# Score columns of a head group dealt to other rounds, and one corner sum read straight from PSUM

## The chip, the cores and the metric

The kernel runs on one core of a Trainium2 chip. The metric is the device time of one execution in microseconds. The profile is one execution taken by the hardware profiler. Its engines are TensorE (PE, with its weight loads as PEld), VectorE (DVE), ScalarE (ACT), GpSimd (POOL) and SyncE (SP).

## The reference

For 8 batches of 8 heads with 576 tokens and head dimension 64, a causal attention with a forget gate is computed, and its output (4608 tokens by 512) goes through a two-layer network with a gelu between.

```python
scores = scale * np.matmul(q, k.transpose(0, 1, 3, 2))
cum = np.cumsum(np.log(np.clip(f, 0.0001, 1.0)), axis=-1)
scores = np.where(causal, -1e9, scores + cum[:, :, :, None] - cum[:, :, None, :])
attn = softmax(scores)
x = np.matmul(attn, v).transpose(0, 2, 1, 3).reshape(B * S, H * D)
h = x @ w_in                       # 512 -> 2048
out = gelu_tanh(h) @ w_out         # 2048 -> 512
```

## The kernel before

**Order of the work.** All work is written out by hand as words in tables (FRONT, SECOND, STEADY, FLUSH, LAST, from L75); each engine gets its instructions in that order. S is a score round, M a mask on POOL, m the same mask on DVE, D the softmax denominators, V the value product, VW and vw the weighting of the values on POOL and DVE, CL a small copy on DVE, LQ and LK loads, TQ and TK transposes on DVE. I, i, Q, E and e are parts of the first layer, F and f steps of the second layer, T and UW sums for both. The tables put F and f steps between the attention's words, so that PE has work while ACT, DVE and POOL finish what the attention needs next.

**Attention.** Four heads of a batch form a head group, `i` from 0 to 15. Keys lie on the partitions, queries on the columns. A score tile for head group i >= 2 has 1536 columns per head, dealt in three rounds of 512 (`rounds`, L50). The list `pieces` (L51) says which columns belong to which key tile: (key tile, first column, first query, number of queries). There are 5 key tiles of 128 keys; the last one is half full. Its 64 keys ("high") share columns 0 to 63 with the 64-column piece "low", which holds the first 64 keys for the first 64 queries in the other half of the partitions. Before the change key tile 0 stands at columns 64 to 575, so that it has 448 columns in round 0 and 64 in round 1.

A round (`scores`, L259) multiplies, for each half `c` of the head dimension and each piece, the four heads one after another, each in its own 32 rows of PE (L277), and ends with two exponentials on ACT into `pt`, 128x1024 each (L285). `mask` (L287) then zeroes the columns above the diagonal with POOL instructions (L291); `mask_by_product` (L311) does it with DVE products by a triangle (L321). `product` (L325) multiplies `pt` by the weights (`denominators`) or by the values (`attn_out`), in the order of key tile 0, low, 1, 2, 3, high (L347). `pt` has two buffers. Head groups 0 and 1 use other tables (`split_pieces`).

**Second layer.** Tokens go in 9 chunks of 512. Chunk 0 is a plain product (`mlp_out`). Chunks 1 to 8 take seven products of blocks instead of eight (`seven_products`, L586). Two PSUM banks, pa and pb, take them in turn; some products add onto what a bank holds. A product that is needed twice is kept in SBUF by a copy on DVE (`keep`, L615, in a pool of three buffers, copy at L617). `result` (L619) sums two parts into an output tile (L624, three buffers) and sends it out on SP's queue. The corner for output block (1,1) stands behind the fifth product:

```python
def corner():
    keep("v4", pa)
    result(1, 1, kept["p7"], kept["v4"])
```

After it come a product into pb and then the last product, which adds onto pa in chunks 1 to 7. In the last chunk (8, `last`) the final product goes to new banks and `piece` adds `kept["v4"]` to it.

Of the kernel before, what the change touches and what calls it, by code (L numbers as in the profile page):

```python
# [16 lines left out]
def kernel(  # L17
# [10 lines left out]
    nc = tc.nc  # L28
# [21 lines left out]
    rounds = [(0, 512), (512, 512), (1024, 512)]  # L50
    pieces = [  # L51
        ("low", 0, 0, 64),
        (0, 64, 64, 512),
        (1, 576, 128, 448),
        (2, 1024, 256, 320),
        (3, 1344, 384, 192),
        ("high", 0, 512, 64),
    ]
# [62 lines left out]
    def many(n, shape, dtype, name):  # L121
        return [singles.tile(shape, dtype, name=f"{name}{i}") for i in range(n)]
# [31 lines left out]
    causal = many(2, [128, 128], BF16, "causal")  # L154
# [8 lines left out]
    for u in range(4):  # L163
        if u not in wsum:
            n = 3 * len([x for x in wsum if x not in UNIT_LIST])
            wsum[u] = [last_w[:, 512 * (n + k):512 * (n + k + 1)].rearrange("p (d n) -> p d n", n=HC) for k in range(3)]

    def gelus(c, ft=0, n=HF):

        half = last_g[ft // HF] if c == NCH - 1 else gT[:, HF * (ft // HF):HF * (ft // HF) + HF]  # L170
        return half[:, ft % HF:ft % HF + n]

    def sums_of(c):
        return (last_s[0], last_s[1], g4) if c == NCH - 1 else (g1, g2, g4)
# [112 lines left out]
    def mask(i, r, keys=None):  # L287
        p = pt[i % 2]

        def keep(x, pattern):  # L290
            nc.gpsimd.affine_select(  # L291
                out=x, in_=x, compare_op=ALU.is_ge,
                fill=0.0, base=0, pattern=pattern, channel_multiplier=-1)

        if i < 2:
            for (key, col, n) in diagonals(r, keys):
                keep(p[:, :, col:col + n], [[0, 4], [1, n]])
            return
        if r == 0:
            keep(p[0:64, :, 0:64], [[0, 4], [1, 64]])  # L300
            keep(p[64:128, :, 0:128].rearrange("p h (b x) -> p h b x", x=64), [[0, 4], [0, 2], [1, 64]])
        for (key, col, q0, nq) in pieces:
            if key in (keys or (1, 2, 3)) and rounds[r][0] <= col < rounds[r][0] + 512:
                keep(p[:, :, col:col + 128], [[0, 4], [1, 128]])

    def diagonals(r, keys):

        return [(4 if key == "high" else key, col, min(nq, 128)) for (key, col, q0, nq) in split_pieces[r]
                if q0 == (512 if key == "high" else 128 * key) and (not keys or (4 if key == "high" else key) in keys)]

    def mask_by_product(i, r, keys=None):  # L311
        p = pt[i % 2]
        if i < 2:
            todo = [(0, col, n) for (key, col, n) in diagonals(r, keys)]
        else:
            todo = [(1 if key == "low" else 0, col, 128) for (key, col, q0, nq) in pieces
                    if (not keys or key in keys) and q0 == 128 * (0 if key == "low" else 9 if key == "high" else key)
                    and rounds[r][0] <= col < rounds[r][0] + 512 and key != 0]
        did = None
        for (m, col, n) in todo:  # L320
            did = nc.vector.tensor_mul(p[:, :, col:col + n], p[:, :, col:col + n],  # L321
                                 causal[m][:, 0:n].unsqueeze(1).to_broadcast([128, 4, n]))
        return did

    def product(i, groups, spare, part=None):  # L325
# [243 lines left out]
    def gelu_sums(half, which=(1, 3, 2, 4), c=0):  # L569

        n = HF // 2
        f0 = slice(n * half, n * half + n)
        g1, g2, g4 = sums_of(c)
        top, low = gelus(c, n * half, n), gelus(c, HF + n * half, n)
        a11, a12, a21, a22 = top[:, :, 0:HC], low[:, :, 0:HC], top[:, :, HC:CH], low[:, :, HC:CH]
        for k in which:
            if k == 1:
                nc.vector.tensor_add(g1[:, f0], a21, a22)
            if k == 2:
                nc.vector.tensor_sub(g2[:, f0], g1[:, f0], a11)  # L580
            if k == 3:
                nc.vector.tensor_sub(a21, a11, a21)
            if k == 4:
                nc.vector.tensor_sub(g4[:, f0], a12, g2[:, f0])

    def seven_products(c):  # L586

        r0, last = CH * c, c == NCH - 1
        g1, g2, g4 = sums_of(c)
        top, low = gelus(c), gelus(c, HF)  # L590
        a11, a12, d1, a22 = top[:, :, 0:HC], low[:, :, 0:HC], top[:, :, HC:], low[:, :, HC:]
        w11, w3 = w_out_sb[:, 0:HF, 0:HD], w_out_sb[:, 0:HF, HD:]
        w21, w22 = w_out_sb[:, HF:, 0:HD], w_out_sb[:, HF:, HD:]

        def multiply(ps, x, w, first, then, ns=range(2), cols=(0, HD)):
            for n in ns:
                for j in range(HF):
                    width = 32 if by_columns else 128
                    for c0 in range(0, 128, width):
                        nc.tensor.matmul(ps[c0:c0 + width, n, cols[0]:cols[1]],  # L600
                                         x[:, j, 128 * n + c0:128 * n + c0 + width],
                                         w[:, j, cols[0]:cols[1]],
                                         start=(first and n == ns[0] and j == 0), stop=(j == HF - 1),
                                         skip_group_check=True)
                    if n == ns[-1] and j == HF - 1:
                        then()
                    yield

        def bank():
            return psM.tile([128, 2, HD], FP32, name="ps_w", tag="m")  # L610

        kept = {}
        copy = nc.scalar.copy if c in ON_ACT else nc.vector.tensor_copy

        def keep(name, ps):  # L615
            kept[name] = snap_pool.tile([128, 2, HD], FP32, name="snap", tag="snap")
            copy(kept[name], ps)  # L617

        def result(i, j, x, y=None):  # L619
            st = ostage_pool.tile([128, 2, HD], FP32, name="o_st", tag="o")  # L620
            if y is None:
                copy(st, x)
            else:
                nc.vector.tensor_add(st, x, y)  # L624
            nc.sync.dma_start(
                out=out[r0 + HC * i:r0 + HC * (i + 1), HD * j:HD * (j + 1)].rearrange("(n p) d -> p n d", p=128),
                in_=st)

        def first_corner():
            result(0, 0, pb, kept["p1"])  # L630
            gelu_sums(1, (3, 4), c)

        def corner():
            keep("v4", pa)
            result(1, 1, kept["p7"], kept["v4"])

        def piece(ps, n, cols):
            st = v_nat[0][:, 0, 4 * n:4 * n + 4, :].rearrange("p h d -> p (h d)")
            s = slice(*cols)
            nc.vector.tensor_add(st[:, s], ps[:, n, s], kept["v4"][:, n, s])  # L640
            eng = nc.scalar if cols[0] else nc.sync
            eng.dma_start(out=out[r0 + 128 * n:r0 + 128 * n + 128, HD + cols[0]:HD + cols[1]], in_=st[:, s])

        pa, pb = bank(), bank()
        yield from multiply(pa, a11, w11, True, lambda: keep("p1", pa))
        yield from multiply(pb, a12, w21, True, first_corner)
        yield from multiply(pa, g2, u2, False, lambda: keep("v2", pa))
        yield from multiply(pb, d1, w3, True, lambda: keep("p7", pb))
        yield from multiply(pa, g1, u1, False, corner)
        yield from multiply(pb, a22, u4, False, lambda: result(1, 0, pb, kept["v2"]))  # L650
        if not last:
            yield from multiply(pa, g4, w22, False, lambda: result(0, 1, pa))
            return
        for n, cols in ((0, (0, HD)), (1, (0, HD // 2)), (1, (HD // 2, HD))):
            ps = bank()
            yield from multiply(ps, g4, w22, True, lambda: piece(ps, n, cols), (n,), cols)
# [94 lines left out]
    def load_values(b, half):  # L751
# [9 lines left out]
        "S": lambda i, r: scores(i, r),  # L761
        "H": lambda i, r, g: scores(i, r, ((2 * g, 2 * g + 1),)),
        "M": lambda i, r, *keys: mask(i, r, keys),
        "m": lambda i, r, *keys: mask_by_product(i, r, keys),
        "D": denominators,
        "V": lambda i, x, *part: attn_out(i, x, False, *part),
# [92 lines left out]
```

## Time and profile before

| | |
|---|---|
| runs | 323.99, 325.89, 326.36 us (median 325.89) |
| span of the profiled execution | 324.3 us; no other time of it is given |
| PE busy | 310.0 us (96%), 5337 matmuls |
| DVE busy | 241.7 us (75%), 374 instructions |
| ACT busy | 212.6 us (66%) |
| POOL busy | 107.0 us (33%) |
| TensorE clock granted | 1.000 of full speed |

The span runs from the first to the last instruction. A busy time is the time in which the engine has at least one instruction under way. Matmuls overlap on PE, so the mean of one matmul is longer than the distance between two starts. Lines like L277 are lines of the kernel before.

### The profile page before, as it was taken

Reading aid. Unit: us, or ns where it says so; the run is one execution under the profiler, and the core shown is the slowest. Engines: PE = TensorE matmul, PEld = TensorE weight load, DVE = VectorE, ACT = ScalarE, POOL = GpSimd, SP = SyncE. Lnnn points to the kernel's source line nnn. Section 1 sums busy time; section 2 is a strip of 40 time slices with the busy share of each in tenths; the row PEclk is TensorE's granted clock in tenths of the full one; section 3 lists DMA queues with packets and bytes.
Section 4 is the critical chain, followed back from the end, with each engine's and each line's share of the span. In section 5 each row is a group of like instructions: output and inputs, shape, how many; then the busy total and the mean of one; then the engine's idle time right before and its main releaser. Section 6 shows DMA issues by size and latency. Waiting matters only on the chain.

```text
span 324.3 us, 11816 instructions
## 1 busy us (share of the span) xinstructions
PE 310.0 (96%) x5337; PEld 221.2 (68%) x5337; DVE 241.7 (75%) x374; ACT 212.6 (66%) x242; POOL 107.0 (33%) x145
## 2 busy tenths in 40 slices
PE   0799989999999999999999999999999999999996
PEld 0557844454677667776788877767776786788785
DVE  3664307998989978779876998599885866597574
ACT  4495667686766786678667876877587743846610
POOL 8868507253111405510752056305610150000000
PEclk9999999999999999999999999999999999999999
DMA  6999999577034951395119610981001011010202
GB/s 117 232 155 165 196 250 217 139 160 143 8 67 88 227 116 36 76 213 107 36 40 211 143 40 6 206 183 35 7 32 67 17 35 53 16 50 2 99 33 98
DMA packets 47490, 33.41 MB, mean 103 GB/s; under 512 B 29776, under 2 KB 42192, under 8 KB 47440
## 3 DMA queue, kind: packets, MB, share of 16 engines
q0 software_dynamic: 9632, 15.99, 28.4%
q1 hardware_dynamic: 37664, 16.60, 18.9%
q8 instruction: 41, 0.67, 0.8%
q14 instruction: 9, 0.07, 0.1%
q10 hardware_dynamic: 144, 0.07, 0.1%
HBM read 36.85 MB, written 9.44 MB: 143 GB/s over the span
## 4 chain that ended last, share of the span: by engine, by line
PE 82%; DMA 6%; POOL 4%; ACT 4%; DVE 2%; issue 1%; POOLq 0%; DVEq 0%
PE ps_w L600 30%; PE ps_h L395 19%; PE po L347 9%; PE ps_q L520 8%; PE ps_s L277 8%; DMA w_out_sb<-in_moe_w_out_dram 4%; PE ps_u L468 4%; PE pso L667 4%; DMA q_c<-in_q_dram 2%; ACT pt L285 2%; POOL pt L291 1%; POOL w_out_sb L201 1%; POOL v_nat L185 1%; POOL w_in_sb L197 1%; PE cum_ps L721 1%
## 5 line engine op out<-in xcount | busy, mean ns | idle before, releaser
L285 ACT ACTIVATE pt<-ps_s 128x1024 bf16<-128x1024 f32 (+2 forms) x100 | 93.9, 990 | 41.3 <-PE ps_s L277 37.1
L291 POOL TENSOR_SCALAR_AFFINE_SELECT pt<-pt 128x512 bf16<-128x512 bf16 (+3 forms) x65 | 40.8, 639 | 98.0 <-ACT pt L285 75.2
L395 PE MATMUL ps_h<-xT,w_in_sb 128*128 128x512 bf16 (+1 forms) x320 | 66.8, 358 | 0.3 <-ACT gT L403 0.2
L395 PEld LDWEIGHTS <-w_in_sb 128*128 128x128 bf16 x320 | 31.2, 98 | 26.7 <-issue 0.6
L600 PEld LDWEIGHTS <-gT 128*32 128x32 bf16 (+1 forms) x1216 | 44.2, 97 | 5.5 <-issue 2.2
L403 ACT ACTIVATE gT<-ps_h 128x1024 bf16<-128x1024 f32 x34 | 34.6, 1017 | 18.7 <-PE ps_h L395 18.4
L600 PE MATMUL ps_w<-w_out_sb,gT 128*32 128x256 bf16 (+1 forms) x1008 | 42.6, 273 | 0.0
L277 PE MATMUL ps_s<-qT,kT 32*128 32x64 bf16 (+5 forms) x896 | 36.3, 263 | 4.6 <-DVE qT L214 4.3
L600 PEld LDWEIGHTS <-gsum 128*32 128x32 bf16 (+1 forms) x948 | 35.5, 97 | 3.6 <-issue 1.3
L231 POOL TENSOR_TENSOR vw<-v_nat,wT 128x1280 bf16<-128x1280 f32 (+1 forms) x13 | 29.6, 2278 | 11.8 <-DMA v_nat<-in_v_dram 11.5
L536 DVE TENSOR_TENSOR usnap<-ps_q,usnap 128x1024 f32<-128x1024 f32 x15 | 17.9, 1222 | 18.6 <-PE ps_q L520 13.2
L277 PEld LDWEIGHTS <-kT 32*128 32x128 bf16 x896 | 16.5, 93 | 20.9 <-issue 11.5
L600 PE MATMUL ps_w<-usum,gsum 128*32 128x256 bf16 (+1 forms) x791 | 29.9, 273 | 0.0
L617 DVE COPY snap<-ps_w 128x512 f32<-128x512 f32 x32 | 21.8, 681 | 6.1 <-PE ps_w L600 6.0
L531 ACT ACTIVATE gT<-usnap 128x1024 bf16<-128x1024 f32 x15 | 15.8, 1054 | 12.1 <-DVE usnap L536 11.8
L379 DVE TENSOR_TENSOR xT<-po,rb 128x576 bf16<-128x576 f32 x26 | 19.5, 752 | 5.6 <-PE po L347 5.3
L347 PE MATMUL po<-pt,vw 128*32 128x64 bf16 (+4 forms) x624 | 22.4, 278 | 0.0
L214 DVE STREAM_TRANSPOSE qT<-q_c 128x576 f32<-128x576 f32 x16 | 19.8, 1247 | 2.7 <-DMA q_c<-in_q_dram 2.5
L214 DVE STREAM_TRANSPOSE kT<-k_c 128x576 f32<-128x576 f32 x16 | 19.5, 1248 | 3.1 <-DMA k_c<-in_k_dram 3.1
L347 PEld LDWEIGHTS <-vw 128*32 128x32 bf16 x672 | 14.8, 97 | 9.3 <-issue 2.8
L208 POOL DMA_DIRECT2D k_c<-in_k_dram x16 | 9.1, 569 | 33.7 <-DVE kT L214 17.4
L520 PEld LDWEIGHTS <-w_in_sb 128*128 128x128 bf16 x160 | 15.6, 98 | 2.5 <-issue 0.4
(134 smaller groups left out, 478.4 us busy)
## 6 DMA issues: line engine op xcount, KB each, us to landing
out_dram<-o_st SPq DMA_DIRECT2D x35, 256.0 KB, 2.3
k_c<-in_k_dram POOLq DMA_DIRECT2D x16, 288.0 KB, 5.2
q_c<-in_q_dram POOLq DMA_DIRECT2D x16, 288.0 KB, 6.2
v_nat<-in_v_dram SPq DMA_DIRECT2D x16, 256.0 KB, 5.3
v_nat<-in_v_dram SPq DMA_DIRECT2D x20, 128.0 KB, 4.9
v_nat<-in_v_dram POOLq DMA_DIRECT2D x8, 256.0 KB, 8.2
w_in_sb<-in_moe_w_in_dram POOLq DMA_DIRECT2D x8, 256.0 KB, 7.6
w_out_sb<-in_moe_w_out_dram POOLq DMA_DIRECT2D x4, 512.0 KB, 11.1
```

Source lines behind the costliest of these rows:

```text
L214: return nc.vector.transpose(out=dst.rearrange("p s c -> p (s c)").bitcast(FP32) .rearrange("p (t a) -> p a t", a=S // 32), in_=src.rearra ...
L231: return eng.tensor_mul(vw[i % 2][:, t0:t1], vb[:, t0:t1, h0:h0 + 4, :], wT[:, i, t0:t1, :].unsqueeze(3).to_broadcast([128, t1 - t0, 4, D]))
L277: nc.tensor.matmul(tiles[h // 2][:, h % 2, c0:c0 + nq], key_columns(i, key, h, c), qq[32 * h:32 * h + 32, q0:q0 + nq, c], start=(c == 0 an ...
L285: nc.scalar.activation(p[:, 2 * g:2 * g + 2, off:off + n], t[:, :, 0:n], AF.Exp, scale=scale)
L291: nc.gpsimd.affine_select(out=x, in_=x, compare_op=ALU.is_ge, fill=0.0, base=0, pattern=pattern, channel_multiplier=-1)
L347: nc.tensor.matmul(po[r0:r0 + w.shape[-1], 448 + q0:448 + q0 + nq], w, p[:, h, col:col + nq], start=(key in (0, "low")), stop=(key in ("lo ...
L379: nc.vector.tensor_mul(xT[:, 2 * u + x, r0 + s0:r0 + s1], po, rbs[i, part])
L395: nc.tensor.matmul(ph[:, j, n * cols:(n + 1) * cols], w_in_sb[:, dt, 128 * ft:128 * ft + 128], xT[:, dt, h0:h0 + cols], start=(dt == 0 and ...
L403: nc.scalar.activation(gelus(c, 2 * pr, 2), ph, AF.Gelu_apprx_tanh)
L520: nc.tensor.matmul(ps[:, k, HC * n:HC * n + HC], w[:, d, 128 * n:128 * n + 128], x[:, d, :], start=(first and n == 0 and d == 0), stop=(d ...
L600: nc.tensor.matmul(ps[c0:c0 + width, n, cols[0]:cols[1]], x[:, j, 128 * n + c0:128 * n + c0 + width], w[:, j, cols[0]:cols[1]], start=(fir ...
L617: copy(kept[name], ps)
```

## The change

Key tile 1 takes columns 64 to 511 and key tile 0 columns 512 to 1023, so that round 1 is key tile 0 and nothing else. Key tile 0's diagonal has a part in the low keys' half of the partitions that needs a mask: its 64 columns by 64 keys stood beside "low" in round 0 and were masked together with it; now they stand in round 1 and get a mask of 64 partitions there. Key tile 1's diagonal mask moves from round 1 to round 0. On POOL, round 0 has three masks instead of two and round 1 one smaller mask; on DVE, round 0 has two products instead of one and round 1 one smaller one. In the second layer the (1,1) corner is summed from PSUM and p7; the copy to v4 stays in the last chunk alone.

```diff
     pieces = [
         ("low", 0, 0, 64),
-        (0, 64, 64, 512),
-        (1, 576, 128, 448),
+        (1, 64, 128, 448),
+        (0, 512, 64, 512),
         (2, 1024, 256, 320),
         (3, 1344, 384, 192),
         ("high", 0, 512, 64),
...
         if r == 0:
-            keep(p[0:64, :, 0:64], [[0, 4], [1, 64]])
-            keep(p[64:128, :, 0:128].rearrange("p h (b x) -> p h b x", x=64), [[0, 4], [0, 2], [1, 64]])
+            for x in (0, 64):
+                keep(p[x:x + 64, :, 0:64], [[0, 4], [1, 64]])
+        if r == 1:
+            keep(p[64:128, :, 512:576], [[0, 4], [1, 64]])
...
-            todo = [(1 if key == "low" else 0, col, 128) for (key, col, q0, nq) in pieces
-                    if (not keys or key in keys) and q0 == 128 * (0 if key == "low" else 9 if key == "high" else key)
-                    and rounds[r][0] <= col < rounds[r][0] + 512 and key != 0]
+            todo = [(1 if key == "low" else 0, col, 64 if key in ("low", 0) else 128) for (key, col, q0, nq) in pieces
+                    if (not keys or key in keys) and key != "high"
+                    and rounds[r][0] <= col < rounds[r][0] + 512]
         did = None
         for (m, col, n) in todo:
-            did = nc.vector.tensor_mul(p[:, :, col:col + n], p[:, :, col:col + n],
-                                 causal[m][:, 0:n].unsqueeze(1).to_broadcast([128, 4, n]))
+            p0 = 64 if (i >= 2 and r == 1) else 0
+            m = 1 if p0 else m
+            did = nc.vector.tensor_mul(p[p0:, :, col:col + n], p[p0:, :, col:col + n],
+                                 causal[m][p0:, 0:n].unsqueeze(1).to_broadcast([128 - p0, 4, n]))
...
         def corner():
-            keep("v4", pa)
-            result(1, 1, kept["p7"], kept["v4"])
+            if last:
+                keep("v4", pa)
+            result(1, 1, pa, kept["p7"])
```

## The prediction

> **What bounds the kernel now.** I read the page's first part, then its chain of work, then the list of what TensorE (PE) waited for.
>
> ```profile
> PE 310.0 (96%) x5337; PEld 221.2 (68%) x5337; DVE 241.7 (75%) x374; ACT 212.6 (66%) x242; POOL 107.0 (33%) x145
> ...
> PE 82%; DMA 6%; POOL 4%; ACT 4%; DVE 2%; issue 1%; POOLq 0%; DVEq 0%
> ```
>
> PE is busy for 310.0 of 324.3 us and carries 82% of the chain that ended last. DVE, which the second half of the change relieves, has 2% of that chain.
>
> ```profile
> PE ps_lt L700 <- POOL utri_f masks.py:66: 4.7, 1, 4.7
> PE ps_s L277 <- DVE qT L214: 4.3, 1, 4.3
> PE pso L667 <- DMA w_out_sb<-in_moe_w_out_dram: 1.3, 2, 0.7
> PE ps_h L395 <- ACT gT L403: 0.2, 1, 0.2
> PE ps_q L520 <- ACT gT L403: 0.2, 1, 0.2
> PE ps_s L277 <- ACT pt L285: 0.2, 1, 0.2
> ```
>
> This is the whole list (us in total, times, longest). The first three rows lie before 47 us, where the change touches one score round at most. From there to the end PE waits 0.6 us in all, and in no row for DVE's second-layer sums (L624) or for POOL's masks (L291). So a microsecond taken off DVE or POOL is worth something only if PE's own sequence gets shorter.
>
> **The score rounds.** One steady iteration in PE's timeline, cut around its first three rounds (round 1 and round 2 of one head group, round 0 of the next):
>
> ```profile
> 155.13 0.64 PE L277 MATMUL ps_s<-qT,kT 32*128 32x64 bf16 x16
> 155.69 0.40 PE L347 MATMUL po<-pt,vw 128*32 128x512 bf16 x4
> ...
> 157.91 0.63 PE L277 MATMUL ps_s<-qT,kT 32*128 32x320 bf16 x16
> 158.47 0.40 PE L347 MATMUL po<-pt,vw 128*32 128x512 bf16 x4
> ...
> 160.91 0.69 PE L277 MATMUL ps_s<-qT,kT 32*128 32x64 bf16 x24
> 161.53 0.40 PE L347 MATMUL po<-pt,w_bf 128*32 128x512 bf16 x4
> ```
>
> A merged row shows only the first shape, so its count matters: round 1 now has 16 matmuls (64 columns for four heads, 448 for four heads, and both again for the other half of the head dimension). The four heads run side by side. From its start to the next work round 1 takes 155.69 - 155.13 = 0.56 us, round 2 also 0.56 us, and round 0, with 24 matmuls, 0.62 us.
>
> The change makes round 1 of each of the 14 head groups i = 2 to 15 eight matmuls of 512 columns. It removes 14 x 8 = 112 matmuls and as many weight loads, but no column: 64 + 448 = 512. What does a group of four 64-column matmuls cost beyond its columns? Round 0 has two such groups more than round 1 and takes 0.06 us longer, 0.03 us each. Streaming alone can be read from the first layer's long run: 64 matmuls of 512 columns in 13.97 us (L395, from 69.14 us), 0.216 us each, so 64 columns are 0.027 us. By this only 2 x 0.003 us a round is saved. On the other hand the starts inside round 1, asked for in narrow windows, put its last group at 155.40, 0.27 us behind the first; streaming of 64 + 448 + 64 columns would be 0.243 us. That is 0.03 us over, and most of it should vanish when two groups remain. I take 0.025 us a round, 14 x 0.025 = 0.35 us. The far end is that the two 64-column groups now cost 0.06 us and become free: 14 x 0.06 = 0.8 us. The trace has no four 512-column matmuls side by side in 32 rows; were they as slow as a single record looks (mean 379 ns for 128x512, against the 216 ns between starts), a round would lose 2 x 0.16 us and the kernel 4.6 us. I reject this end because the 448-column groups show a mean of 357 ns and yet follow each other within 0.20 us. Rounds 0 keep their shapes (64, 448, 64), round 2 is untouched, and the ScalarE exponentials keep size and number.
>
> **The masks.** POOL's timeline for the same iteration:
>
> ```profile
> 155.10 1.13 POOL L291 TENSOR_SCALAR_AFFINE_SELECT pt<-pt 64x256 bf16<-64x256 bf16 x2 [7.31 <-ACT spare L245]
> 156.32 2.33 POOL L231 TENSOR_TENSOR vw<-v_nat,wT 128x1280 bf16<-128x1280 f32 x1
> 158.61 1.09 POOL L291 TENSOR_SCALAR_AFFINE_SELECT pt<-pt 128x512 bf16<-128x512 bf16 x1
> 160.65 1.22 POOL L291 TENSOR_SCALAR_AFFINE_SELECT pt<-pt 128x512 bf16<-128x512 bf16 x2 [0.95 <-ACT pt L285]
> 161.84 2.33 POOL L231 TENSOR_TENSOR vw<-v_nat,wT 128x1280 bf16<-128x1280 f32 x1
> ```
>
> From the groups by shape: 64x256 takes 409 ns, 64x512 705 ns, 128x512 694 ns. Round 0's masks go from 409 + 705 to 409 + 409 + 694 ns (+0.40 us, 12 head groups on POOL), round 1's from 694 to 409 ns (-0.285 us, 10 head groups). POOL gains 12 x 0.40 - 10 x 0.285 = 1.9 us of 107. What is queued behind them: vw (156.32) starts 0.40 us later and ends at 159.05 instead of 158.65; its readers are CL on DVE at 160.27 and the value product at 163.3. Round 1's mask then ends at 159.5 instead of 159.7. Round 2's masks wait for ScalarE until 160.65 anyway. The loads of q and k behind the last masks start as before, since that is a round-2 mask too, waiting for ScalarE; only in FRONT do a few start up to 0.4 us later, and their transposes come several words further on. In FRONT six masks stand on DVE: four of round 1 shrink from 448 ns to something between 224 ns (the 64x256 copy of L236) and 448 ns, two of round 0 gain a product between the same ends. That is 2 x 0.448 = +0.9 us at worst and (2 - 4) x 0.224 = -0.45 us at best; I take -0.45, the copy being nearest in size, and it lies off PE's sequence.
>
> **A wait that moves.** The denominator and value products begin with key tile 0. Now its first product needs round 0's masks; afterwards it needs round 1's mask. In the steady iteration that product starts at 161.53 (the last row of the rounds above) and the mask is done by 159.5: 2.0 us spare. In FRONT and FLUSH two or more pieces of work also lie between. Cost: nothing, covered by those pieces.
>
> **The (1,1) corner.** By shape, mean ns as the second number behind the bar:
>
> ```profile
> L617 DVE COPY snap<-ps_w 128x512 f32<-128x512 f32 x32 | 21.8, 681 | 6.1 <-PE ps_w L600 6.0
> L624 DVE TENSOR_TENSOR o_st<-ps_w,snap 128x512 f32<-128x512 f32 x16 | 10.9, 683 | 2.6 <-PE ps_w L600 2.5
> L624 DVE TENSOR_TENSOR o_st<-snap 128x512 f32<-128x512 f32 x8 | 6.3, 788 | 0.3
> ```
>
> In chunks 1 to 7 copy and sum (681 + 788 ns) become one sum from PSUM (683 ns): 7 x 0.786 = 5.5 us off DVE. The bank pa, which the copy freed 0.68 us after PE's last matmul, is freed by the sum, also 0.68 us long and standing where the copy stood. The sum also waits for its output buffer; before, that wait followed the copy, and the 0.3 us of idle time in front of the eight sums says that it cost nothing. In chunk 8 the copy stays and the sum follows it, so pa is free about 0.7 us later; the 16 matmuls into pb, 1.75 us, stand between, and the sum ends at 319.05 where PE needs the bank at 319.18. Cost 0, at worst 0.1 us. DVE's 5.5 us are covered by PE, which does not wait for DVE after 10 us.
>
> **Sum.** -0.35 us (rounds) + 0 + 0 = 324.3 - 0.35 = 323.9 us of span in the profiled execution. No separate time of that execution is given; the runs shown are 323.99, 325.89 and 326.36 us, median 1.6 us above its span. I carry this over: **325.5 us**.
>
> **Rivals.**
> *Weight loads exposed.* If each 64-column group really cost its weight load (93 ns, mean of the L277 loads), 14 x 2 x 0.093 = 2.6 us would go: 323.3 us. For it: the many short loads. Against it: round 0's two extra groups cost 0.03 us each, not 0.09. [...]
>
> *DVE is on the path after all.* If PE's short pauses at tile changes hid DVE waits, the 5.5 us of the corner and 0.45 us of masks would come through: 325.5 - 5.95 = 319.6 us. For it: by stretches DVE is busy for 31.7 of the 35.0 us between 69 and 104 us, and on some corners V's product waits for DVE behind them. Against it: no row of PE's waits names DVE after 10 us, and PE is busy for all of each steady iteration.
>
> *The products wait for round 1's mask (slower).* The first product of D moves its need for this mask ahead by key tile 0's and the low piece's 0.216 + 0.027 = 0.24 us. Were POOL the last to finish in every head group, each would lose these 0.24 us and POOL's net 0.115 us: 14 x 0.36 = 5.0 us, 325.5 + 5.0 = 330.5 us. It decides once round 1's mask ends more than 2.0 us later than computed. For it: a vw of 2.33 us that waits for a value load stands ahead of the mask on POOL. Against it: that margin, and today's key tile 1 product, which has this need already, shows no wait.
>
> **How the numbers follow.** Forecast 0.79, weight loads 0.05, DVE 0.06, mask wait 0.07, something unseen on the slow side 0.03. About 1% is what a measurement of this kernel tells from no change; the three runs spread over 0.7%. Forecast and weight loads lie within it, DVE is faster, the last two are slower. So faster 0.06, same 0.84, slower 0.10. The range holds the first two with the spread of the runs: the likeliest's own is 323.2 to 326.4 (the terms' 0 to 0.8 us and the runs' -1.9 and +0.5 us); I stretch it to 322.8 and, for part of the mask wait, 327.8.
>
> **What would show it.** Right: L277 has 784 PE matmuls (896 - 112); round 1 starts the next work 0.53 to 0.55 us later; of the corner's lines (L617, L624 of the kernel before) the sum that reads only SBUF is gone and 25 copies stay; DVE is near 236 us and POOL near 109 us; PE's waits after 47 us stay under 1 us. Wrong: a row PE po L347 <- POOL pt L291, a round 1 longer than 0.56 us, or a span that falls by the microseconds that DVE lost.

## The result and the profile after

The changed kernel is slower. Its median is 330.21 us (329.71 to 331.09, 5 runs) against 325.11 us (323.99 to 326.36, 5 runs) for the kernel before: a ratio of 1.0157, 95% interval 1.0132 to 1.0182. The spans of the two profiled executions are 328.4 and 324.3 us. The prediction said 325.5 us and a range up to 327.8, so it was wrong in sign and in range. The medians and ratios below leave out three of f4's twelve executions, 329.4 to 331.5 us, which the record counts as slow; f4's trace is of one of them and isn't used.

In the kernel after, lines from L321 on have moved by 4 (from L636 on by 5): the products (L347) are L351, DVE's mask products (L321) L325, the transposes and the scaling (L366, L370, L379) L370, L374, L383, the first layer (L395) L399, the second layer (L600, L617, L624) L604, L621, L628. First the page: busy time of each engine, and the chain that ended last by engine.

```profile
PE 311.5 (95%) x5225; PEld 219.1 (67%) x5225; DVE 239.9 (73%) x369; ACT 212.7 (65%) x242; POOL 109.2 (33%) x157
...
PE 81%; DMA 6%; POOL 4%; ACT 4%; DVE 3%; issue 1%; POOLq 0%
```

The 112 matmuls are gone (5337 to 5225), yet PE is busy for 1.5 us longer, and DVE has 3% of the chain instead of 2%. The list of what PE waited for (us in total, times, longest) has a new second row:

```profile
PE ps_lt L705 <- ACT f_all L700: 4.8, 1, 4.8
PE po L351 <- DVE pt L325: 2.9, 1, 2.9
PE ps_s L277 <- DVE qT L214: 2.8, 1, 2.8
```

One single product waits 2.9 us for one of DVE's mask products. The steady iterations are as planned. Round 1 of a head group is now 8 matmuls of 512 columns; PE's timeline (start, us, group) shows one and the product behind it:

```profile
158.16 0.63 PE L277 MATMUL ps_s<-qT,kT 32*128 32x512 bf16 x8
158.72 0.87 PE L351 MATMUL po<-pt,vw 128*32 128x512 bf16 x24
```

It takes 158.72 - 158.16 = 0.56 us, as the 16 matmuls did. The corner, by shape (the second number behind the bar is the mean in ns):

```profile
L621 DVE COPY snap<-ps_w 128x512 f32<-128x512 f32 x25 | 16.9, 678 | 3.2 <-PE ps_w L604 3.1
L628 DVE TENSOR_TENSOR o_st<-ps_w,snap 128x512 f32<-128x512 f32 x24 | 16.4, 683 | 5.9 <-PE ps_w L604 5.9
```

There are 25 copies instead of 32, 24 sums from PSUM instead of 16, and the sums from SBUF alone are gone. One steady iteration takes the same 33.6 us in both traces (151.34 to 184.96 us before, 154.37 to 187.98 after).

**Where the time went.** I divide both traces at the same four events and compare the stretches, in us:

| stretch | before | after | difference |
|---|---|---|---|
| start of the span to the product of chunk 0 (`pso`) on PE in FRONT that waits for the last part of its weights | 46.86 | 45.62 | -1.24 |
| from there to D.3's first denominator transpose (DVE `den`) | 18.80 | 21.93 | +3.13 |
| from there to the next first-layer matmul (`ps_h`) | 3.48 | 4.57 | +1.09 |
| from there to PE's end, then to DVE's last sum | 252.54 | 252.46 | -0.08 |
| DVE's last sum to the end of the span | 2.59 | 3.85 | +1.26 |

The first row is no work of the change: its length varies from 43.3 to 46.9 us over the kernels of this study that have the same code there. Two places lose time: some 4.2 us about D.3 in FRONT, and 1.3 us in the tail, behind all computing.

**The first place.** DVE's and POOL's timelines (us of start, us of length; the bracket names a wait), with the product of D.3 on PE at the end. Before:

```profile
62.44 0.53 POOL L208 DMA_DIRECT2D k_c<-in_k_dram  x1 [7.78 <-ACT pt L285]
62.90 0.22 DVE L236 COPY vw<-vw 64x256 bf16<-64x256 bf16 x1
63.02 1.40 POOL L291 TENSOR_SCALAR_AFFINE_SELECT pt<-pt 128x512 bf16<-128x512 bf16 x2
63.15 0.78 DVE L321 TENSOR_TENSOR pt<-pt,causal 128x512 bf16<-128x512 bf16 x1
64.73 0.86 PE L347 MATMUL po<-pt,w_bf 128*32 128x512 bf16 x24
```

and after:

```profile
61.39 0.53 POOL L208 DMA_DIRECT2D k_c<-in_k_dram  x1 [7.53 <-DVE kT L214]
61.71 4.39 DVE L236 COPY vw<-vw 64x256 bf16<-64x256 bf16 x1
61.93 1.23 POOL L291 TENSOR_SCALAR_AFFINE_SELECT pt<-pt 128x512 bf16<-128x512 bf16 x2
63.10 0.55 POOL L208 DMA_DIRECT2D q_c<-in_q_dram  x1
63.66 2.34 POOL L231 TENSOR_TENSOR vw<-v_nat,wT 128x1280 bf16<-128x1280 f32 x1
66.13 0.29 DVE L325 TENSOR_TENSOR pt<-pt,causal 64x256 bf16<-64x256 bf16 x1
66.47 0.87 PE L351 MATMUL po<-pt,w_bf 128*32 128x512 bf16 x24 [2.92 <-DVE pt L325]
```

The same small copy, CL.3, takes 0.22 us before and 4.39 us after. It starts 0.32 us behind the start of POOL's load issue (LK.6) and ends at 66.10, 0.10 us after POOL has finished the masks M.3.2, the issue LQ.6 and the weighting VW.4 (63.66 + 2.34 = 66.00). Behind the copy on DVE stands m.3.1, and D.3 on PE needs it.

Then PE's clock drops. By windows, the columns are the stretch, its length, the busy time and count of PE, PEld, DVE, ACT and POOL, the granted clock, the DMA share and GB/s:

```profile
63.00:66.40 3.40, 0.55 (x8) 0.30 (x9) 3.37 (x2) 1.68 (x2) 2.98 (x3) 1.00 0.95 156
66.40:70.00 3.60, 3.53 (x76) 1.94 (x79) 2.90 (x5) 1.66 (x2) 0.59 (x1) 0.65 0.26 28
70.00:72.00 2.00, 2.00 (x44) 0.95 (x35) 1.45 (x3) 0.28 (x1) 1.45 (x3) 0.77 0.69 125
```

PE is busy for 0.55 of 3.40 us, and in the next 5.6 us it is granted 0.65 and 0.77 of its clock; before, the same three windows show 1.00, here the second:

```profile
66.40:70.00 3.60, 3.50 (x73) 1.91 (x66) 3.43 (x7) 2.78 (x3) 2.49 (x4) 1.00 0.67 114
```

Narrower windows of after, in the same columns, show the slow stretch by itself:

```profile
67.20:67.60 0.40, 0.40 (x24) 0.23 (x16) 0.40 (x2) 0.00 (x0) 0.00 (x0) 0.87 0.10 17
67.60:70.80 3.20, 3.20 (x62) 1.55 (x62) 2.37 (x5) 1.94 (x2) 1.00 (x2) 0.50 0.48 65
70.80:71.20 0.40, 0.40 (x20) 0.30 (x12) 0.13 (x1) 0.00 (x0) 0.37 (x1) 0.87 0.96 179
```

The clock is at half from about 67.5 to 70.9 us, 3.4 us in all, and it falls 1.0 us after PE went on with D.3 at 66.47. In this stretch the +1.09 us of the table arise. The wait ahead of it is 2.92 us long by the row of PE's waits. In e8 below, with a wait of 2.9 us too, the clock is at half for 6.8 us (the mean granted clock of its profiled execution is 0.987, against 0.992 here); e5, f2, g4 and h1, where D.3 isn't held for long, have 0.997 to 1.000. What sets the length of the slow stretch is not shown.

**The second place.** The output transfers of the tail, first after (windows 320 to 329 us, the row of the instruction queue and of the output tile, median us to landing):

```profile
q8 instruction: 1, 0.02, 1.1%
...
out_dram<-o_st SPq DMA_DIRECT2D x2, 256.0 KB, 4.0
```

then before (318 to 325 us), where no row of that queue exists:

```profile
out_dram<-o_st SPq DMA_DIRECT2D x2, 256.0 KB, 2.1
```

One packet of 0.02 MB on the instruction queue q8 falls among the last output transfers, 1.3 us ahead of PE's end, and they need about twice as long to land.

### The profile page after: what moved, and what is told of

The parts are those of the page before. It is cut to its first block, busy times and chain, and to the rows that moved or that the text cites. A ratio compares the mean times of both kernels' runs of the same rounds, so it can differ in the third digit from the quotient of the medians.

```text
span 328.4 us, 11611 instructions
## 1 busy us (share of the span) xinstructions
PE 311.5 (95%) x5225; PEld 219.1 (67%) x5225; DVE 239.9 (73%) x369; ACT 212.7 (65%) x242; POOL 109.2 (33%) x157
## 4 chain that ended last, share of the span: by engine, by line
PE 81%; DMA 6%; POOL 4%; ACT 4%; DVE 3%; issue 1%; POOLq 0%
PE ps_w L604 30%; PE ps_h L399 19%; PE po L351 9%; PE ps_q L524 8%; PE ps_s L277 7%; DMA w_out_sb<-in_moe_w_out_dram 4%; PE ps_u L472 4%; PE pso L672 3%; ACT pt L285 2%; DMA q_c<-in_q_dram 2%; DVE vw L236 1%; POOL pt L291 1%; PE cum_ps L726 1%; POOL w_out_sb L201 1%; POOL v_nat L185 1%
## 5 line engine op out<-in xcount | busy, mean ns | idle before, releaser
L291 POOL TENSOR_SCALAR_AFFINE_SELECT pt<-pt 64x256 bf16<-64x256 bf16 (+2 forms) x77 | 43.1, 570 | 97.1 <-ACT pt L285 73.3
L399 PE MATMUL ps_h<-xT,w_in_sb 128*128 128x512 bf16 (+1 forms) x320 | 66.8, 358 | 0.3 <-ACT gT L407 0.2
L399 PEld LDWEIGHTS <-w_in_sb 128*128 128x128 bf16 x320 | 31.2, 98 | 26.7 <-issue 0.6
L604 PEld LDWEIGHTS <-gT 128*32 128x32 bf16 (+1 forms) x1216 | 44.0, 97 | 5.6 <-issue 2.2
L604 PE MATMUL ps_w<-w_out_sb,gT 128*32 128x256 bf16 (+1 forms) x1008 | 42.6, 273 | 0.0
L277 PE MATMUL ps_s<-qT,kT 32*128 32x64 bf16 (+6 forms) x784 | 36.5, 280 | 3.1 <-DVE qT L214 2.8
L604 PEld LDWEIGHTS <-gsum 128*32 128x32 bf16 (+1 forms) x948 | 35.3, 97 | 4.9 <-issue 2.4
L604 PE MATMUL ps_w<-usum,gsum 128*32 128x256 bf16 (+1 forms) x791 | 29.8, 273 | 0.0
L277 PEld LDWEIGHTS <-kT 32*128 32x128 bf16 x784 | 14.8, 94 | 18.3 <-issue 11.4
L383 DVE TENSOR_TENSOR xT<-po,rb 128x576 bf16<-128x576 f32 x26 | 19.6, 753 | 6.4 <-PE po L351 6.2
L351 PE MATMUL po<-pt,vw 128*32 128x64 bf16 (+4 forms) x624 | 23.0, 284 | 0.0
L351 PEld LDWEIGHTS <-vw 128*32 128x32 bf16 x672 | 14.8, 99 | 11.5 <-issue 5.1
L628 DVE TENSOR_TENSOR o_st<-ps_w,snap 128x512 f32<-128x512 f32 x24 | 16.4, 683 | 5.9 <-PE ps_w L604 5.9
L208 POOL DMA_DIRECT2D k_c<-in_k_dram x16 | 9.1, 569 | 33.6 <-DVE kT L214 25.0
L621 DVE COPY snap<-ps_w 128x512 f32<-128x512 f32 x25 | 16.9, 678 | 3.2 <-PE ps_w L604 3.1
```

The source lines that it names most:

```text
L277: nc.tensor.matmul(tiles[h // 2][:, h % 2, c0:c0 + nq], key_columns(i, key, h, c), qq[32 * h:32 * h + 32, q0:q0 + nq, c], start=(c == 0 an ...
L291: nc.gpsimd.affine_select(out=x, in_=x, compare_op=ALU.is_ge, fill=0.0, base=0, pattern=pattern, channel_multiplier=-1)
L351: nc.tensor.matmul(po[r0:r0 + w.shape[-1], 448 + q0:448 + q0 + nq], w, p[:, h, col:col + nq], start=(key in (0, "low")), stop=(key in ("lo ...
L383: nc.vector.tensor_mul(xT[:, 2 * u + x, r0 + s0:r0 + s1], po, rbs[i, part])
L399: nc.tensor.matmul(ph[:, j, n * cols:(n + 1) * cols], w_in_sb[:, dt, 128 * ft:128 * ft + 128], xT[:, dt, h0:h0 + cols], start=(dt == 0 and ...
L604: nc.tensor.matmul(ps[c0:c0 + width, n, cols[0]:cols[1]], x[:, j, 128 * n + c0:128 * n + c0 + width], w[:, j, cols[0]:cols[1]], start=(fir ...
```

## The experiments

Of the tables, only the words about the change are shown; `...` stands for code that isn't shown.

**Parts of the change.** With the old corner put back (e1), and with the new corner alone in the kernel before (e2):

```diff
# e1, against after
-            if last:
-                keep("v4", pa)
-            result(1, 1, pa, kept["p7"])
+            keep("v4", pa)
+            result(1, 1, kept["p7"], kept["v4"])
# e2, against before: the same lines the other way round
```

> The changed kernel with the old corner (copy to v4, sum from SBUF); columns and masks as changed. Theory A (the loss is one copy of head group 3's values on DVE, CL.3, that is locked out for 4.4 us while POOL works without a pause, set off by the longer round-0 mask on DVE): the corner first comes at 99 us, long after the stall, so the loss stays whole: 329 to 331 us, one vw<-vw copy of about 4.4 us. Rival B (the corner's sum holds its bank longer and costs a little in each of 7 chunks): about 325 us. Rival C (key tile 0's moved need for round 1's mask costs in each head group): 330 us too, but with PE waits on masks in several head groups.

Measured: 330.65 us, ratio 1.0168 (1.0123 to 1.0213); the copy takes 4.39 us again.

> The kernel before with the new corner alone. Theory A: no stall, all vw<-vw copies near 0.22 us, 324 to 326 us, as before: DVE's 5.5 us less are worth nothing. Rival B: 329 to 331 us. Rival C: 325 us.

Measured: 324.70 us, ratio 0.9994 (0.9968 to 1.0019); the copy takes 0.22 us. So the whole loss comes with the columns, and the corner's 5.5 us of DVE are worth nothing.

**Is it the copy, or whatever DVE starts there?** CL.3 is moved ahead of the transpose TK.4, so that m.3.1 stands in its place:

```diff
# e3, against after
-  m.3.0 S.3.2 TK.4 LK.6@LQ.4 f.0.1 f.0.3 V.2.1 M.3.2 f.0.2 S.4.1 CL.3 m.3.1 LQ.6
+  m.3.0 S.3.2 CL.3 TK.4 LK.6@LQ.4 f.0.1 f.0.3 V.2.1 M.3.2 f.0.2 S.4.1 m.3.1 LQ.6
```

> The changed kernel, with the word CL.3 moved ahead of TK.4, into a stretch where POOL is idle; every instruction is kept. Theory A: the copy takes 0.22 us, D.3 does not wait, and the time falls to 324.5 to 326 us. Rival B: still 330 us. Rival C: still 328 us or more, since D.3 needs the same mask as before.

Measured: 329.61 us, ratio 1.0144 (1.0112 to 1.0176). The time expected of a freed copy was missed. The copy is free, but now DVE's timeline has

```profile
61.59 4.47 DVE L325 TENSOR_TENSOR pt<-pt,causal 64x256 bf16<-64x256 bf16 x1
```

at the same distance behind LK.6's start (61.28), and PE waits 2.7 us for it. It isn't the copy; it is the place.

**Is it the new masks' form?** In e6 (e3's order) and e8 (after's order) m.3.1 covers all 128 partitions; in e7 the kernel before gets the half mask. (So e6 and e8 zero too much in head group 3, and e7 leaves a part of key tile 1's mask out; the order of the instructions stays.)

```diff
# e6 and e8
-            p0 = 64 if (i >= 2 and r == 1) else 0
+            p0 = 64 if (i >= 2 and i != 3 and r == 1) else 0
# e7, in before
-            did = nc.vector.tensor_mul(p[:, :, col:col + n], p[:, :, col:col + n],
+            p0, n = (64, 64) if (i == 3 and r == 1) else (0, n)
+            did = nc.vector.tensor_mul(p[p0:, :, col:col + n], p[p0:, :, col:col + n],
...
```

> As e3_copy_earlier, but head group 3's mask m.3.1 covers all 128 partitions by 64 columns (it zeroes too much in that head group). Theory A1 (it is the form: an instruction on partitions 64 to 127 alone is held by a busy POOL, one on all partitions only slowed): the mask takes 0.3 to 0.9 us and the time is 325 to 327 us. Theory A2 (it is the moment of the start, in POOL's load issue with masks right behind): held for 4.4 us as in e3, 329 to 331 us.

Measured: 329.1 us, ratio 1.0118 (1.0071 to 1.0165); the full mask starts 0.21 us behind LK.6's start and takes 4.56 us.

> The kernel before, with head group 3's mask m.3.1 on partitions 64 to 127 and 64 columns only (so the mask of key tile 1 is incomplete in that head group). CL.3 and the mask start at the moments of the kernel before. Theory A1 (form): the mask, or the copy ahead of it, is held until POOL pauses, 3.5 to 4.5 us, and the time rises to 328 to 330 us. Theory A2 (moment): the copy takes 0.22 us, the mask under 1 us, 325 us.

Measured: 325.7 us, ratio 0.9999 (0.9967 to 1.003); nothing is held, the half mask takes 0.65 us beside POOL's masks.

> The changed kernel with m.3.1 on all 128 partitions by 64 columns and CL.3 where it was (the mask zeroes too much in head group 3). Theory A1 in the form that the pair of copy and half mask, both on partitions 64 to 127, is what is held: no stall, 325 to 327 us. Theory A2 (moment of the copy): the copy is held for 4.4 us again, 329 to 331 us.

Measured: 330.22 us, ratio 1.0153 (1.0118 to 1.0187); the copy is held for 4.39 us. The form of m.3.1 doesn't matter.

**Is it the moment at which DVE starts?** The kernel after has m.3.0 as two products (0.62 us instead of 0.41), which puts DVE's later work elsewhere against POOL's. The kernel before gets m.3.0 in two and in three products:

```diff
# e4, in before; f3: three products, (1, 0, 64), (1, 64, 32), (1, 96, 32)
+        if i == 3 and r == 0:
+            todo = [(1, 0, 64), (1, 64, 64)]
...
```

> The kernel before, with only head group 3's round-0 mask on DVE cut in two products of 64 columns: the same result, about 0.2 us more of DVE ahead of CL.3, columns as before. Theory A in its sharp form (a shift of DVE against POOL by a tenth of a microsecond is enough to put the copy under POOL's load issue and masks): one vw<-vw copy of 2 to 5 us and 328 to 331 us. If the shift alone is not enough: 325 us, and something else in the changed columns sets the stall off. Rivals B and C: 325 us.

Measured: 324.74 us, ratio 1.0012 (0.9981 to 1.0043). The copy starts 0.38 us behind LK.6's start and takes 0.22 us.

> The kernel before with m.3.0 in three products (64, 32 and 32 columns; same result), so that CL.3 starts some 0.32 us behind the start of POOL's load issue, as in the changed kernel, while the mask behind the issue still starts after a gap of 0.05 us. Theory A3 (the gap decides: in it the waiting DVE instruction gets through): the copy takes 0.22 us, 325 us. Theory A4 (the moment within the issue decides): the copy is held for about 4.4 us, 328 to 330 us.

Measured: 324.68 us, ratio 0.9985 (0.9964 to 1.0005). The copy starts at +0.32 us, exactly as in after, and takes 0.23 us:

```profile
61.84 0.53 POOL L208 DMA_DIRECT2D k_c<-in_k_dram  x1 [7.91 <-ACT pt L285]
62.16 0.23 DVE L236 COPY vw<-vw 64x256 bf16<-64x256 bf16 x1
62.42 1.51 POOL L291 TENSOR_SCALAR_AFFINE_SELECT pt<-pt 128x512 bf16<-128x512 bf16 x2
```

The moment alone isn't the cause, and neither is the issue: the copy runs beside it at its usual length. What differs: here and in before, POOL's first mask starts at +0.58 us, 0.05 us behind the end of the issue (0.53 us long); in after it starts at +0.54, with at most 0.01 us between. Nor does the copy have to be done before the mask starts: in before it starts 0.12 us ahead of the mask and ends 0.10 us behind the mask's start (62.90 + 0.22 against 63.02), unheld; in after it starts 0.22 us ahead (61.71 against 61.93) and is held.

**Does POOL's run of work hold it?** VW.4, 2.34 us of the run, is moved behind LQ.7:

```diff
# e5, against after
-  H.4.0.0 VW.4 V.3.1 v.3.0 f.0.1 H.4.2.0 U.0 m.4.1 LV.2.1@m.3.1 I.1.1 LQ.7@CL.3 I.1.4
+  H.4.0.0 V.3.1 v.3.0 f.0.1 H.4.2.0 U.0 m.4.1 LV.2.1@m.3.1 I.1.1 LQ.7@CL.3 VW.4 I.1.4
```

> The changed kernel with VW.4 (2.34 us on POOL, not needed before head group 4's values) behind the load LQ.7, so that POOL pauses after masks and LQ.6. Theory A (a DVE instruction that comes while POOL is busy without a pause is held until POOL pauses; in the changed kernel that is 4.4 us after its start): it is now held for about 2.0 us instead of 4.4, D.3 waits for 0.3 to 0.7 us instead of 2.9, and the time is 325 to 327 us. Rival D (the held instruction waits for something else, whose end only falls together with POOL's): still 4.4 us and 330 us.

Measured: 326.16 us, ratio 1.0043 (1.0019 to 1.0067). DVE's and POOL's timelines:

```profile
62.96 1.53 DVE L236 COPY vw<-vw 64x256 bf16<-64x256 bf16 x1
63.18 1.23 POOL L291 TENSOR_SCALAR_AFFINE_SELECT pt<-pt 128x512 bf16<-128x512 bf16 x2
```

The copy now ends at 64.49, 0.08 us after the masks (64.41), and D.3 hardly waits. The hold follows POOL's work: shorter work, shorter hold. It also passes while POOL issues LQ.6 (64.35 to 64.90), which follows the masks at once. In the kernel after, the same issue, with VW.4 ready behind it, let nothing through.

**A pause by an extra wait.** Two kernels give POOL's first mask in M.3.2 a further wait, on an event long past, in the hope of the 0.05 us pause: on the load LQ.5 (g1), and on an older mask of POOL's own (g3).

```diff
# g1, against after; g3: after(did, dmas["mask"]), with dmas["mask"] = did at i == 2
...
+                if i == 3 and key == 2:
+                    after(did, dmas["LQ.5"])
```

> The changed kernel with one more wait on the first mask of M.3.2 (for the load LQ.5, landed long before), so that POOL again has a gap of about 0.05 us between the issue of LK.6 and that mask. Theory A3 (in the gap the waiting DVE instruction gets through): the copy CL.3 takes 0.22 us, D.3 does not wait, and the time falls to 325.5 to 326.5 us though a wait was added. Theory A4 (the moment within the issue decides): the copy is held for 4.4 us again, 329.5 to 331 us.

Measured: 329.81 us, ratio 1.0141 (1.0092 to 1.0191).

> The changed kernel with one more wait on the first mask of M.3.2, for an older mask of POOL itself (done 7 us before), so that it has the pair of waits of the kernel before. Theory A3 (the DVE instruction that came during the issue gets through in the gap between issue and mask): the mask starts 0.05 us behind the issue's end, the copy CL.3 takes 0.22 us, D.3 does not wait, 325.5 to 326.5 us. Theory A4 (the offset within the issue decides, or something else): the copy is held for 4.4 us, 329 to 331 us.

Measured: 329.63 us, ratio 1.0139 (1.01 to 1.0178). In both, the mask still starts at +0.53 to +0.54 us, no pause appears, and the copy is held for 4.39 us. They say nothing on the pause, since they made none. A wait that surely makes one is on the copy itself:

```diff
# h1, against after
-  V.2.1 M.3.2 f.0.2 S.4.1 CL.3 m.3.1 LQ.6
+  V.2.1 CL.3 M.3.2 f.0.2 S.4.1 m.3.1 LQ.6
...
+                if i == 3 and key == 2:
+                    after(did, dmas["CL.3"])
```

> Kernel after, with one wait added in FRONT: POOL's first mask of M.3.2 starts only when DVE's copy CL.3 has ended. The copy still starts about 0.32 us behind the start of LK.6's issue; nothing else of DVE's or POOL's order changes. Theory P (the copy is held because POOL goes from the issue into its masks without a pause, and goes on for 4 us): the wait makes a pause, the copy takes 0.2 to 0.4 us, POOL's masks start about 0.1 us later than before, PE's row po <- DVE pt shrinks from 2.9 to under 0.5 us, and of the 4.6 us about 4 go, the tail's 1.2 us stay, give or take one: 325.0 to 326.6 us. Rival I (the load issue itself, or what it sets going, holds the copy until some later event): the copy stays long, POOL's masks wait with it, and the time stays at 329 us or above.

Measured: 326.01 us, ratio 1.0035 (1.0017 to 1.0053). The timelines of DVE and POOL (L327 is m.3.1 here):

```profile
61.08 0.53 POOL L208 DMA_DIRECT2D k_c<-in_k_dram  x1 [7.51 <-DVE kT L214]
61.40 0.23 DVE L236 COPY vw<-vw 64x256 bf16<-64x256 bf16 x1
61.66 0.29 DVE L327 TENSOR_TENSOR pt<-pt,causal 64x256 bf16<-64x256 bf16 x1
61.77 1.26 POOL L291 TENSOR_SCALAR_AFFINE_SELECT pt<-pt 128x512 bf16<-128x512 bf16 x2 [0.16 <-DVE vw L236]
```

The copy starts at the same +0.32 us, behind the same issue, and with a pause of 0.16 us on POOL it takes 0.23 us. The product m.3.1 behind it isn't held either, though it starts 0.11 us ahead of the mask and POOL then works without a pause for 4 us. So starting inside the issue isn't enough; it takes POOL's masks (and what follows them) coming on without a pause.

**Taking DVE's work out of the place.** Both m.3.1 and CL.3 are put ahead of TK.4:

```diff
# f2, against after
-  m.3.0 S.3.2 TK.4 LK.6@LQ.4 f.0.1 f.0.3 V.2.1 M.3.2 f.0.2 S.4.1 CL.3 m.3.1 LQ.6
+  m.3.0 V.2.0 m.3.1 CL.3 S.3.2 TK.4 LK.6@LQ.4 f.0.1 f.0.3 V.2.1 M.3.2 f.0.2 S.4.1 LQ.6
```

(V.2.0, which stood ahead of m.3.0, now stands behind it.)

> The changed kernel with m.3.0 ahead of V.2.0 and with m.3.1 and CL.3 ahead of TK.4, so that no DVE instruction of this kind starts in POOL's load issue and masks. Theory A: no hold, D.3 does not wait, about 4.2 us less than the changed kernel: 325.5 to 326.5 us, the rest over the kernel before being the 1.2 us at the end (theory T). Rival C (the moved need for the mask costs in itself): D.3 still waits, 328 us or more.

Measured: 325.92 us, ratio 1.0041 (1.002 to 1.0062). In the place stands now the transpose of q, which starts 0.21 us behind LK.6's start and takes 1.23 us, no longer than elsewhere (1.25).

e5, f2 and h1 end the long hold in three ways, and all three leave 0.35 to 0.43%, 1.1 to 1.4 us. That is the tail: DVE's last sum to the end is 3.84, 3.38 and 3.98 us there, against 2.59 before.

**The tail.** The page of before counts 41 fetches (0.67 MB, some 16 KB each) on the instruction queue q8, against 10674 PE instructions, some 260 for each; counted in the trace of before from one fetch to the next, it is 253 PE instructions on the mean of 40 distances and 177 to 312 on single ones. Near the end they lie some 15 us apart. That they fetch PE's instructions is read from f1 and g2 below, where matmuls added on PE alone move the last one. The kernel after has 224 PE instructions fewer (112 matmuls, 112 weight loads), so the fetch that lies at 306.2 us before, 15.1 us ahead of PE's end, falls 1.3 us ahead of it. If so, adding a few matmuls to the kernel before must bring a fetch into its tail, too. `keep_busy` runs dummy matmuls of 64 columns in the first microseconds, ahead of FRONT:

```diff
# f1, in before; g2: keep_busy(10, 64)
+        keep_busy(16, 64)
```

> The kernel before with 16 more 64-column matmuls (32 PE instructions with their weight loads) in the first microseconds, where PE is idle. Theory T (the 1.2 us at the very end: every 256 PE instructions a 16 KB instruction fetch goes out, and the changed kernel, 224 instructions shorter, has its last fetch between the last output transfers, which then land late): 32 more instructions put the fetch of the kernel before at the same place, so from DVE's last sum to the end 3.2 to 4.0 us instead of 2.6, output transfers landing in 3.3 to 4.3 us instead of 2.1, and the time about 326 us, 1.0 to 1.5 us above the kernel before. Rival U (the late end follows from the changed columns, masks or the corner): 2.6 us, 325 us.

Measured: 324.44 us, ratio 0.9988 (0.9974 to 1.0001). A miss: though 32 more PE instructions are, by the 256 of the expectation (253 measured on the mean, single distances further off), the same place as 224 fewer, the fetch comes 2.0 us ahead of PE's end and meets only the first output transfer, which lands in 2.65 instead of 2.14 us; the others land within 0.2 us of before, and DVE's last sum to the end is 2.61 us.

> The kernel before with 10 more 64-column matmuls (20 PE instructions) in the first microseconds. Theory T: the last instruction fetch now starts 1.2 to 1.5 us ahead of PE's end, as in the changed kernel, output transfers land in 3.2 to 4.3 us, and from DVE's last sum to the end it takes 3.3 to 4.0 us instead of 2.6: 325.5 to 326.5 us. Rival U: 2.6 us, 324.5 to 325.2 us.

Measured: 325.69 us, ratio 1.0022 (0.9996 to 1.0047). The fetch now lies at 320.8 us, 0.7 us behind PE's end and so later than expected. Four of five output transfers land in 3.4 to 4.4 us, and DVE's last sum to the end takes 4.46 us in the profiled execution, 1.87 more than before. The timed runs give 0.7 us, with zero just inside the interval; the profile shows the mechanism, the times don't settle its size. Over the traces the tail grows as the fetch moves back: 2.0 us ahead of PE's end it is 2.61 us (f1), 1.9 ahead 3.18 (e1), 1.3 ahead 3.38 (f2) and 3.85 (after), 0.7 behind 4.46 (g2). A second instruction queue, q14, with 8 KB in some tails, isn't the cause: e2 and g4 have it among the last output transfers and a tail of 2.59 us, and in g2, whose tail is long, it lies 4.3 us ahead of PE's end.

**Both at once.** f4 is f2 with 112 dummy matmuls, as many as the change removed; g4 is f2 with 20, enough to push the fetch ahead of the transfers:

```diff
# g4, against f2; f4: keep_busy(56, 64) at two places
+        keep_busy(20, 64)
```

> f2 with 112 more 64-column matmuls in the first microseconds, so that PE has as many instructions as in the kernel before (10653 rows). Theories A and T together: no hold, 2.6 us from DVE's last sum to the end, and the time of the kernel before within 0.3%: 324 to 325.5 us. If another part of the change cost or brought something, it would be left here.

Measured: 324.79 us, ratio 1.0005 (0.998 to 1.0031).

> f2 (no hold) with 20 more 64-column matmuls in the first microseconds, which move the last instruction fetch some 2 us ahead, before the last output transfers. Theories A and T together: about 2.6 us from DVE's last sum to the end and 324.3 to 325.3 us, the time of the kernel before within 0.3%. If the rest of the change were worth the forecast 0.35 us or more, it would show as a ratio under 1.

Measured: 324.95 us, ratio 1.0001 (0.9982 to 1.002). The fetch falls between 316 and 317 us, the first output transfer starts at 319.0, and the tail is 2.59 us. With both places mended the changed kernel costs what the kernel before costs: these two explain the whole loss, about 3.8 us by the hold with its clock loss (1.0157 less some 1.004), about 1.2 us by the tail. What is left of the change is worth nothing that can be measured; no kernel of the study is faster than before clear of the noise (f1 comes nearest, 0.9974 to 1.0001).

## Why the prediction was wrong

- **The moved wait and the masks in FRONT: the failed step.** "In FRONT and FLUSH two or more pieces of work also lie between. Cost: nothing, covered by those pieces", and of DVE's masks: "it lies off PE's sequence". The margin of 2.0 us was read in a steady iteration, where POOL makes the mask. In FRONT, DVE makes it; in the trace of before m.3.1 ended at 63.93 and D.3 started at 64.73, a margin of 0.8 us that I didn't read. More important, a table's order doesn't say when two engines' instructions meet. DVE's copy ahead of m.3.1 met a POOL run without its 0.05 us pause and was held, which brought 4.2 us: 3.1 us up to D.3's transpose (2.9 of them the wait on PE) and 1.1 us by the lower clock behind it. The moved need by itself cost nothing: in f2 and h1 D.3 begins with the same mask, and PE's list has no wait for it. Whether the longer m.3.0 had a part in it isn't shown; put into the kernel before (e4, f3), it held nothing.
- **The rival of the mask wait** had the sign and the product (D) right, and its time, 330.5 us, is near the 330.21 measured. That is a coincidence: it put 0.36 us on each of 14 head groups and on POOL's masks, while the loss fell on a single head group through DVE. Its sign "PE po <- POOL pt" never appeared; PE po L351 <- DVE pt L325 did. "PE's waits after 47 us stay under 1 us" failed by this row.
- **Score rounds, -0.35 us: mis-sized.** From start to start, the 14 rounds 1 last 0.563 to 0.567 us before and 0.558 to 0.563 us after. Their means are 0.004 us apart, 0.06 us for 14: near the low end in the working (2 x 0.003 us, from streaming), not the 0.025 us that I took from a single round's inner starts. The 0.53 to 0.55 us named as the sign of being right were not reached. The weight-load rival falls with it.
- **The corner: right.** 25 copies remain, and e2's 0.9994 shows that DVE's time was covered. That rules out the rival in which DVE was on the path. DVE's 239.9 us less the 4.17 us of the hold (4.39 - 0.22) are 235.7, against 236 predicted; POOL's 109.2 against 109; L277 has 784 matmuls.
- **The end of the kernel** had no term in the sum at all. That instruction fetches exist could be read before: the page counts 41 of them on q8. What else used the DMA engines in the last 5 us was not asked. It cost about 1.2 us.

**What stays open.** That POOL's masks and weighting, one close behind the other, hold the DVE instruction is shown by e5 and h1. Not shown is by what rule it gets its turn: beside LQ.6's issue in e5, not in after; nor that a pause of 0.05 us is by itself what lets it through, since only h1 made a pause in a kernel with the new columns, and a longer one. Not shown either is why POOL's first mask follows the issue with no pause in every kernel with the new columns (h1 apart), and 0.05 us or a little more behind it in all with the old ones (before, e4, e7, f3 and others): the waits added in g1 and g3 didn't change it. Nor is it clear how DVE's m.3.1 in before (0.78 us; the same shape takes 0.42 us in f3) gets its turn between the two masks.

## What to carry to other kernels

When a change shifts small DVE work against POOL, look in every stage, the hand-written prologue first, for stretches in which POOL goes from one instruction to the next without a pause (here some 4 us, beside which a copy of 0.22 us took 4.39), and ask which DVE copy or product starts inside, and who on the critical engine waits behind it. A margin holds for the stage and the engine in which it was read (here 2.0 us in a steady iteration and 0.8 us in FRONT). With 224 PE instructions fewer, the last instruction fetch fell 1.3 us ahead of PE's end instead of 15.1 us, so when a kernel loses instructions the last microseconds of DMA deserve a look of their own, and gains of a tenth of a per cent are smaller than both effects (about 3.8 and 1.2 us of 325 here).

## What the runs showed of the hardware

- A DVE copy of 0.22 us (before) took 4.39 us (after), and a product of 0.29 us (after) 4.47 us (e3), or 4.56 us on all 128 partitions (e6), while POOL ran an issue, two masks, an issue and a weighting with no more than 0.01 us between them; the copy ended 0.10 us behind the last of these five (after), and after 1.53 us, 0.08 us behind the masks, where no weighting followed the second issue (e5). With a pause of 0.05 us (f3) or 0.16 us (h1) it took 0.23 us. A DVE transpose that started in the same place was not held (f2, 1.23 us).
- PE was granted half its clock for 3.4 us (after), from 1.0 us behind the end of a wait of 2.9 us; the stretch from D.3's transpose to the first layer took 1.1 us longer, on top of the 3.1 us.
- A 16 KB instruction fetch among the last output transfers, 256 KB and less, raised their landing from 1.6 to 2.2 us (before) to 2.3 to 4.3 us (after), and the tail from 2.59 to 3.85 us. In the list of PE's waits (after) no fetch shows; the cost lies with the output transfers of the tail.
